# Reordering and padding the SBUF pools of a fused attention and two-MLP kernel so that the fp32r matmul operands lie at one address modulo 512 bytes

## The chip, the cores and the metric

The kernel runs on one NeuronCore of a Trainium2 chip. The metric is the device time of one execution in microseconds (us), from the chip's own clock; the median of several runs counts. TensorE is called PE, VectorE DVE, ScalarE ACT, GpSimd POOL, and SyncE SP.

## What is computed

The reference is causal attention with a sliding window and a few sink keys, followed by two MLPs without residuals. All inputs are float32.

```python
# q, k, v: (2, 8, 768, 64); n_sink 4, window 128
scores = q @ k.T / 8, kept where key < n_sink or 0 <= query - key < window, else -1e9
a = softmax(scores);  x = (a @ v) as (1536, 512)
h = x @ w_in                      # 512 -> 2048
x = (relu(h) ** 2) @ w_out        # 2048 -> 512
h = x @ w_in2
P = a0 + a1*h + a2*h**2 + a3*h**3
Q = 1 + |b0|*|h| + |b1|*h**2
out = (P / (Q + 1e-6)) @ w_out2
```

## The kernel before

**Precision.** Nearly every matrix product is made of three matmuls of type fp32r. Each operand is split into a high part (the value rounded to fp32r) and a low part (what is left of it), and the sum hi·hi + lo·hi + hi·lo is accumulated in PSUM. So a weight tile `w` becomes `whi` and `wlo`, the activations `x` become `xhi` and `xlo`, the hidden values `g` become `ghi` and `glo`, and the input `y` of the second MLP becomes `yhi` and `ylo`.

**Stages.** Tokens go through attention and the first MLP in four groups (`GROUPS`) of 512, 256, 256 and 512 tokens. While the MLP of one group runs on PE, the attention of the next group is woven into it (`slot`, `tick`). The last group has no attention beside it. Then the second MLP runs over three tiles of 512 tokens.

For each of the 16 blocks `f` of 128 hidden features, `gemm1_part` (L445 to L447) makes `h` with a 128x128 piece of the weights as the stationary operand, which PE loads before the matmul, and the activations as the moving operand, which streams through it: 12 matmuls of n columns, where n is the group's token number or 512. In the first MLP `gemm2a` (L468, L469, L472) follows, again with weights stationary and `ghi` or `glo` moving: 12 matmuls of n columns. In the second MLP `gemm2b` (L503 to L505) has it the other way round: pieces of `ghi` and `glo` are stationary, and the weights, 512 columns, are moving. Every one of these matmuls loads its stationary operand anew, and the load for a matmul is made while the matmul before it streams.

All in all there are 1,920 such matmuls of 512 columns and 768 of 256 columns. From the first matmul of the last token group to the end of the program PE has 1,548 matmuls, of which 1,536 have 512 columns and 12 have 256, left over from the third group.

**Order.** The order of the instructions on each engine is fixed when the program is built: by the scheduler, or, for PE in the two groups of 256 tokens, by the order of the code. In the part that runs here, this order is the same before and after the change on every engine, and so are the semaphores that each instruction waits for. (The two programs differ only in waits of the class `General`, a fallback for other inputs that does not run here.)

**Where tiles lie.** SBUF tiles come from pools, which are laid out one behind the other: `const` (masks, small constants) first, then `wp` (all 64 weight tiles of 2,048 bytes per partition), `stage` (raw weights from HBM, `st`; float32 weights, `wt`), `yp` (y, and early attention inputs), `xp` (`xhi`, `xlo`) and `gp` (`ghi`, `glo`) from the left, `att` (attention) and later `ysp` (`yhi`, `ylo` of the first and third tile; those of the second tile are in `xp`) from the right. A tile of `stage` with tag `st` is 4,104 bytes long, and three of them stand in a row, so what comes behind `stage` lies at another place modulo 512 than what comes before it. Slices of an operand step by 512 bytes (a piece of stationary operand), 1,024 or 2,048 bytes, so that each slice lies at its tile's address modulo 512.

Of the kernel before, what the change touches and what calls it, by code (L numbers as in the profile page):

```python
# [10 lines left out]
F32 = mybir.dt.float32  # L11
# [8 lines left out]
P = 128  # L20
# [27 lines left out]
TAIL = 3  # L48
HP = 60
NTOP = 1  # L50
IAD = 3
ST_T = 5
ST_PV = 2
# [18 lines left out]
def units():  # L72
    out = []
    for g, segs in enumerate(GROUPS):
        for h in range(H):
            xo = 0
            for seg in segs:
                out.append((g, h, seg, xo))
                xo += seg[2] * P
    return out  # L80
# [40 lines left out]
def to_f32(nc, st, t, top):  # L121

    mid = st.bitcast(I32)[:, 1 : 1 + 2 * WH].rearrange("p (n w) -> p n w", w=2)[:, :, 0]
    head = st.bitcast(BF16)[:, 4 : 4 + 4 * WH].rearrange("p (n w) -> p n w", w=4)[:, :, 0]
    nc.scalar.copy(top.bitcast(F16).rearrange("p (n w) -> p n w", w=2)[:, :, 1], head)  # L127
    nc.vector.scalar_tensor_tensor(t.bitcast(I32), in0=mid, scalar=13, in1=top,  # L128
                                   op0=ALU.logical_shift_right, op1=ALU.bitwise_or)
# [20 lines left out]
class Fast:  # L150
# [17 lines left out]
    def setup(self):  # L168
        nc, c = self.nc, self.const
        self.zero = c.tile([P, P], BF16, name="zero")  # L170
        nc.gpsimd.memset(self.zero, 0.0)
        self.tops = [c.tile([P, WH], I32, name=f"top{i}") for i in range(NTOP)]
        self.conv_i = 0
        for top in self.tops:
            nc.gpsimd.memset(top, 0)
        self.ident = c.tile([P, P], F32, name="ident")
        self.nsw = c.tile([P, 4], I32, name="nsw")
        self.nswf = c.tile([P, 4], F32, name="nswf")
        self.par = c.tile([P, 2], F32, name="par")
        ab = c.tile([P, 6], F32, name="ab")  # L180
        self.ab = ab
        io = self.io
        nc.scalar.dma_start(self.nsw, io["nsw"].bitcast(I32).partition_broadcast(P))
        nc.scalar.dma_start(ab[:, 0:4], io["a"].partition_broadcast(P))
        nc.scalar.dma_start(ab[:, 4:6], io["bb"].partition_broadcast(P))
        make_identity(nc, self.ident)
        rel = self.wp.tile([P, WH], F32, tag="whi4_0", name="rel")[:, :P]
        col = self.wp.tile([P, WH], F32, tag="wlo4_0", name="col")[:, :P]
        nc.gpsimd.iota(rel, pattern=[[-1, P]], base=0, channel_multiplier=1,
                       allow_small_or_imprecise_dtypes=True)  # L190
        nc.gpsimd.iota(col, pattern=[[1, P]], base=0, channel_multiplier=0,
                       allow_small_or_imprecise_dtypes=True)
        v = nc.vector
        f = self.nswf
        t = c.tile([P, 2], F32, name="neg")
        v.tensor_copy(f, self.nsw)
        lo = f.rearrange("p (s w) -> p s w", w=2)[:, :, 0:1]
        hi = f.rearrange("p (s w) -> p s w", w=2)[:, :, 1:2]
        t3 = t.rearrange("p (s w) -> p s w", w=1)
        p3 = self.par.rearrange("p (s w) -> p s w", w=1)  # L200
        v.tensor_scalar(t3, lo, 0.0, 4294967296.0, op0=ALU.is_lt, op1=ALU.mult)
        v.tensor_tensor(t3, t3, lo, op=ALU.add)
        v.scalar_tensor_tensor(p3, in0=hi, scalar=4294967296.0, in1=t3, op0=ALU.mult, op1=ALU.add)
        ns, win = self.par[:, 0:1], self.par[:, 1:2]
        self.m0 = c.tile([P, P], F32, name="m0")
        self.m1 = c.tile([P, 2 * P], F32, name="m1")
        self.m2 = c.tile([P, KB + P], F32, name="m2")
        self.nabs = c.tile([P, 2], F32, name="nabs")
        m0, m1, m2 = self.m0, self.m1, self.m2
        tmp = lambda tag: self.wp.tile([P, WH], F32, tag=tag, name="tmp")[:, :P]  # L210
        out, fut, rel1 = tmp("whi4_1"), tmp("wlo4_1"), tmp("whi5_0")
        v.tensor_scalar(fut, rel, 0.0, BIG, op0=ALU.is_lt, op1=ALU.mult)
        v.tensor_scalar_add(rel1, rel, 128.0)
        cur, prv = m2[:, KB : KB + P], m2[:, 0:P]
        v.tensor_scalar(cur, rel, win, BIG, op0=ALU.is_ge, op1=ALU.mult)
        v.tensor_tensor(cur, cur, fut, op=ALU.max)
        v.tensor_scalar(out, col, ns, BIG, op0=ALU.is_ge, op1=ALU.mult)
        v.tensor_tensor(m0, cur, out, op=ALU.min)
        v.tensor_scalar(prv, rel1, win, BIG, op0=ALU.is_ge, op1=ALU.mult)
        v.tensor_tensor(m1[:, 0:P], prv, out, op=ALU.min)  # L220
        v.tensor_copy(m1[:, P : 2 * P], cur)
        v.tensor_copy(m2[:, P:KB], out[:, :NSK])
        nu = sum(u[2][2] for u in units())
        self.mn = c.tile([P, nu], F32, name="mn")
        self.mn_i = 0


    def alt_tags(self, alt):
# [27 lines left out]
    def att_unit(self, u, raws, alt):  # L256
# [11 lines left out]
        at = self.att  # L268
# [19 lines left out]
            A.copy(vst[:, :, 0:D], vr3)  # L288
            G.tensor_tensor(vst[:, :, D : 2 * D], vr3, vst[:, :, 0:D].bitcast(F32), op=ALU.subtract)
        yield  # L290
        ps, sums = [], at.tile([P, 4], F32, tag="sums", name="sums", bufs=6)
        for i in range(nb):
            blk = blk0 + i
            if pv:
# [74 lines left out]
        c, half = h // 2, h % 2  # L369
# [43 lines left out]
    def w_split(self, which, f, half):  # L413
        with ExitStack() as c:
            if which == 0 and self.va_hist:
                for op in self.va_hist[-min(len(self.va_hist), 1 + IAD)]:
                    if op is not None:
# [3 lines left out]
    def w_split_(self, which, f, half):  # L421
        nc = self.nc
        st = self.wst.pop((which, f, half))
        t = self.stage.tile([P, WH], F32, tag="wt", name="wt", bufs=2)
        to_f32(nc, st, t, self.tops[self.conv_i % NTOP])
        self.conv_i += 1
# [81 lines left out]
    def run(self, ctx):  # L508
# [5 lines left out]
        mk = lambda c, name, bufs, side, **kw: c.enter_context(  # L514
            tc.tile_pool(name=name, bufs=bufs, side=side, reuse_waits="tile", **kw))
        root = ctx
        self.wp = mk(root, "wp", 1, "left")
        self.stage = mk(root, "stage", 1, "left")
        self.yp = mk(root, "yp", 1, "left")
        self.psum = mk(root, "psum", 1, None, space=bass.MemoryType.PSUM)  # L520
        self.att_banks, self.h_banks = [0, 1, 2, 3, 6, 7], [4, 5]
# [6 lines left out]
        sx = ExitStack()  # L528
        self.xp = mk(root, "xp", 1, "left")
        self.gp = mk(sx, "gp", 3, "left")  # L530
        sa = ExitStack()
        self.att = mk(sa, "att", 1, "right")

# [467 lines left out]
```

## Time and profile before

| | |
|---|---|
| median of 3 runs | 687.15 us (686.5 to 687.27) |
| the profiled execution's own time | 687.72 us |
| its span, first to last instruction | 685.8 us |
| PE busy | 661.7 us, 96% of the span |
| DVE / ACT / POOL busy | 509.8 / 475.6 / 164.0 us |
| granted PE clock, mean | 0.990 of full speed |

The span is what the trace covers; about 1.9 us of the execution lie around it. A row of the timeline is one instruction, or several of one line that follow each other, with its start and its duration. Matmuls overlap: the next one starts long before the one before it has ended, so what a matmul costs in a dense stretch is the distance from its start to the next start, not its duration. That distance is called its spacing here.

### The profile page before, as it was taken

The page shows a single profiled execution, that of the slowest core. Times are in us where ns is not written, and L with a number is a line of the kernel's source. Part 1 is how long each engine was busy: PE and PEld are TensorE (multiplying, and loading weights), DVE is VectorE, ACT ScalarE, POOL GpSimd, SP SyncE. Part 2 cuts the span into 40 slices and gives each one's busy share as a digit, 9 for nine tenths or more (in the row PEclk, how much of TensorE's full clock was granted, in tenths as well). Part 3 has the DMA queues.
Part 4 walks back from the last instruction along what each step waited for, and adds up shares of the span by engine and source line. Part 5 has one row for each costly group of instructions (what it writes and reads, how often), then busy time and mean ns, then how long its engine had stood idle before and what let it go on. Part 6 is the DMA issues. An engine that isn't in the chain of part 4 may idle for free.

```text
span 685.8 us, 10158 instructions
## 1 busy us (share of the span) xinstructions
PE 661.7 (96%) x3433; PEld 545.6 (80%) x3433; DVE 509.8 (74%) x1068; ACT 475.6 (69%) x1044; POOL 164.0 (24%) x174
## 2 busy tenths in 40 slices
PE   5999999999799999999999999999999999999995
PEld 3656787778699989999888888888888888888884
DVE  6886777778588887876566639998778778777772
ACT  4876977778677776766677758777666666666662
POOL 3553111111223232323000001353223332222221
PEclk9999999999799999999999999999999999999999
DMA  7761655445322222200456530000010000000001
GB/s 284 249 197 41 183 177 163 153 155 170 110 76 87 87 63 84 87 9 1 156 185 191 189 108 1 0 1 0 1 62 0 1 0 1 32 31 1 0 1 66
DMA packets 25403, 58.41 MB, mean 85 GB/s; under 512 B 3200, under 2 KB 9600, under 8 KB 25344
## 3 DMA queue, kind: packets, MB, share of 16 engines
q1 hardware_dynamic: 24768, 57.55, 26.4%
q8 instruction: 29, 0.48, 0.3%
q14 instruction: 30, 0.25, 0.1%
q10 hardware_dynamic: 576, 0.14, 0.1%
HBM read 54.53 MB, written 3.15 MB: 84 GB/s over the span
## 4 chain that ended last, share of the span: by engine, by line
PE 72%; DVE 0%; ACT 0%; issue 0%
PE b L445 11%; PE b L446 11%; PE b L447 11%; PE b L503 7%; PE b L505 7%; PE b L504 7%; PE b L468 4%; PE b L472 4%; PE b L469 4%; PE b L366 2%; PE b L303 2%; PE b L332 1%; PE b L357 1%; PE b L336 1%; PE b L656 0%
## 5 line engine op out<-in xcount | busy, mean ns | idle before, releaser
L445 PE MATMUL b<-xhi,whi 128*128 128x512 f32 (+1 forms) x320 | 112.5, 356 | 1.1 <-ACT xhi L374 0.8
L446 PE MATMUL b<-xlo,whi 128*128 128x512 f32 (+1 forms) x320 | 113.1, 354 | 0.0
L447 PE MATMUL b<-xhi,wlo 128*128 128x512 f32 (+1 forms) x320 | 112.5, 351 | 0.0
L494 POOL TENSOR_TENSOR glo<-t,ghi 128x512 fp32r<-128x512 f32 x34 | 45.0, 1323 | 220.4 <-ACT ghi L493 202.6
L468 PE MATMUL b<-ghi,whi 128*128 128x512 f32 (+1 forms) x256 | 77.8, 344 | 0.3 <-ACT b L456 0.3
L469 PE MATMUL b<-ghi,wlo 128*128 128x512 f32 (+1 forms) x256 | 76.8, 339 | 0.0
L504 PE MATMUL b<-wlo,ghi 128*128 128x512 f32 x192 | 76.0, 396 | 0.0
L503 PE MATMUL b<-whi,ghi 128*128 128x512 f32 x192 | 75.8, 396 | 0.0
L505 PE MATMUL b<-whi,glo 128*128 128x512 f32 x192 | 73.2, 396 | 0.0
L445 PEld LDWEIGHTS b<-xhi,whi 128*128 128x128 f32 x320 | 60.6, 190 | 9.8 <-ACT xhi L374 1.0
L447 PEld LDWEIGHTS b<-xhi,wlo 128*128 128x128 f32 x320 | 60.7, 190 | 9.0 <-DVE wlo L430 0.5
L446 PEld LDWEIGHTS b<-xlo,whi 128*128 128x128 f32 x320 | 60.9, 190 | 8.2
L282 POOL TENSOR_TENSOR klo<-raw,khi 128x448 fp32r<-128x448 f32 (+1 forms) x32 | 33.8, 1056 | 128.7 <-PE b L303 113.4
L430 DVE TENSOR_TENSOR wlo<-wt,whi 128x512 fp32r<-128x512 f32 x64 | 44.8, 700 | 24.7 <-ACT whi L429 24.3
L309 ACT ACTIVATE p<-p,mn 128x288 f32<-128x288 f32 (+2 forms) x96 | 48.3, 503 | 19.2 <-DVE mn L307 18.6
L429 ACT CAST whi<-wt 128x512 fp32r<-128x512 f32 x64 | 39.4, 616 | 29.0 <-PE b L446 23.2
L472 PE MATMUL b<-glo,whi 128*128 128x512 f32 (+1 forms) x256 | 57.0, 340 | 0.2 <-DVE glo L457 0.2
L307 DVE CUSTOM_DVE_ANT_0 p<-b,m 128x288 f32<-128x288 f32 (+2 forms) x96 | 39.6, 419 | 21.5 <-PE b L303 20.4
L128 DVE SCALAR_TENSOR_TENSOR wt<-st,top 128x512 int32<-128x512 int32 x64 | 48.1, 752 | 6.5 <-ACT top L127 4.7
L469 PEld LDWEIGHTS b<-ghi,wlo 128*128 128x128 f32 x256 | 47.8, 188 | 5.7 <-DVE wlo L430 0.5
L468 PEld LDWEIGHTS b<-ghi,whi 128*128 128x128 f32 x256 | 47.5, 188 | 5.8 <-ACT b L456 0.6
L445 PE MATMUL b<-yhi,whi 128*128 128x512 f32 x128 | 50.7, 396 | 0.0
(151 smaller groups left out, 1554.3 us busy)
## 6 DMA issues: line engine op xcount, KB each, us to landing
st<-w SPq DMA_DIRECT2D x64, 512.0 KB, 3.8
raw<-att SPq DMA_DIRECT2D x24, 352.0 KB, 2.9
rawv<-att SPq DMA_DIRECT2D x32, 128.0 KB, 2.4
raw<-att SPq DMA_DIRECT2D x12, 256.0 KB, 3.6
raw_e<-att SPq DMA_DIRECT2D x8, 352.0 KB, 4.6
out<-o SPq DMA_DIRECT2D x8, 256.0 KB, 2.3
rawv<-att SPq DMA_DIRECT2D x16, 64.0 KB, 2.7
raw_e<-att SPq DMA_DIRECT2D x4, 256.0 KB, 5.0
```

The source lines that it names most:

```text
L128: nc.vector.scalar_tensor_tensor(t.bitcast(I32), in0=mid, scalar=13, in1=top, op0=ALU.logical_shift_right, op1=ALU.bitwise_or)
L309: self.lastA = A.activation(pt[:, :w], pt[:, :w], AF.Exp, scale=-1.0, bias=mn, accum_out=sums[:, i : i + 1])
L445: nc.tensor.matmul(h[:, :n], whi[:, cs], xhi[:, c, :n], start=(c == 0), stop=False)
L446: nc.tensor.matmul(h[:, :n], whi[:, cs], xlo[:, c, :n], start=False, stop=False)
L447: nc.tensor.matmul(h[:, :n], wlo[:, cs], xhi[:, c, :n], start=False, stop=(c == NC - 1))
L468: nc.tensor.matmul(acc[m], whi[:, ms], ghi, start=(f == 0 and not pk), stop=pk, **kw)
L469: nc.tensor.matmul(acc[m], wlo[:, ms], ghi, start=False, stop=pk, **kw)
L472: nc.tensor.matmul(acc[m], whi[:, ms], glo, start=False, stop=pk or f == NF - 1, **kw)
L494: self.lastL = nc.gpsimd.tensor_tensor(glo, t3, ghi.bitcast(F32), op=ALU.subtract)
L503: nc.tensor.matmul(acc[t], ghi[:, ts_], whi, start=(f == 0), stop=False)
L504: nc.tensor.matmul(acc[t], ghi[:, ts_], wlo, start=False, stop=False)
L505: nc.tensor.matmul(acc[t], glo[:, ts_], whi, start=False, stop=(f == NF - 1))
```

## The change

```diff
+PAD = 128
 ...
 # Fast.setup
         self.mn = c.tile([P, nu], F32, name="mn")
         self.mn_i = 0
+        c.tile([P, PAD // 4], F32, name="pad")
 ...
 # Fast.att_unit
-        ps, sums = [], at.tile([P, 4], F32, tag="sums", name="sums", bufs=6)
+        ps, sums = [], self.const.tile([P, 4], F32, tag="sums", name="sums", bufs=6)
 ...
 # Fast.run
         self.wp = mk(root, "wp", 1, "left")
-        self.stage = mk(root, "stage", 1, "left")
         self.yp = mk(root, "yp", 1, "left")
 ...
         self.xp = mk(root, "xp", 1, "left")
         self.gp = mk(sx, "gp", 3, "left")
+        self.stage = mk(sx, "stage", 1, "left")
```

A tile of 128 bytes that nothing uses is put behind the constants, the six small `sums` tiles (32 bytes apart) move from `att` to `const`, and the pool `stage` moves behind `gp`. No instruction is added, removed or moved. What changes is where tiles lie. From the allocation of the two built programs, addresses in a partition modulo 512:

| operand | before | after |
|---|---|---|
| `whi`, `wlo` (all weight tiles) | 160 | 480 |
| `xhi`, `xlo`; `yhi`, `ylo` of the second tile | 256 | 480 |
| `ghi`, `glo` | 256 | 480 |
| `yhi`, `ylo` of the first and third tile | 480 | 480 |
| attention `khi`, `vst`, `pst`, `pthi`, `ptlo` | 480 | 480 |
| attention `klo` | 224 | 224 |
| attention `qst` | 288 | 480 |
| attention `raw` (two buffers) | 288, 32 | 480, 224 |
| attention `p` (four buffers) | 480, 96, 224, 352 | the same |
| `st` (three buffers) | 160, 192, 224 | 480, 0, 32 |
| `wt` | 256 | 64 |

## Rows read from the trace of the kernel before

**Rows 1.** The page: PE's busy time, and the span in 40 slices.

```profile
PE 661.7 (96%) x3433; PEld 545.6 (80%) x3433; DVE 509.8 (74%) x1068; ACT 475.6 (69%) x1044; POOL 164.0 (24%) x174
...
PE   5999999999799999999999999999999999999995
...
PEclk9999999999799999999999999999999999999999
```

**Rows 2.** Busy time of each engine by stretch (us); instructions in brackets; PE clock.

```profile
core 0: us, PE busy (x) PEld busy (x) DVE busy (x) ACT busy (x) POOL busy (x), PEclk, DMA share, GB/s
...
70.00:171.70 101.70, 100.80 (x483) 80.30 (x482) 78.70 (x168) 80.21 (x174) 13.84 (x14) 1.00 0.54 166
171.70:184.30 12.60, 8.16 (x34) 6.97 (x34) 6.28 (x24) 7.36 (x21) 2.44 (x4) 0.59 0.39 119
184.30:318.50 134.20, 133.05 (x1077) 127.79 (x1076) 103.09 (x304) 93.97 (x285) 36.29 (x41) 1.00 0.22 66
318.50:409.60 91.10, 91.10 (x398) 73.61 (x397) 55.46 (x82) 62.32 (x111) 5.73 (x4) 1.00 0.49 156
409.60:678.10 268.50, 268.50 (x1153) 216.60 (x1151) 213.89 (x301) 182.11 (x314) 75.96 (x60) 1.00 0.02 9
...
440.00:480.00 40.00, 40.00 (x173) 32.27 (x172) 37.32 (x51) 30.95 (x56) 17.85 (x15) 1.00 0.00 1
```

**Rows 3.** The timeline of PE: first matmul of the last token group, last of all.

```profile
318.46 0.48 PE L445 MATMUL b<-xhi,whi 128*128 128x512 f32 x1
...
678.09 0.40 PE L505 MATMUL b<-whi,glo 128*128 128x512 f32 x1
```

**Rows 4.** Timeline, moving operand at 256, weights at 160: first and last of 43 starts.

```profile
330.06 0.39 PE L447 MATMUL b<-xhi,wlo 128*128 128x512 f32 x1
...
339.86 0.39 PE L445 MATMUL b<-xhi,whi 128*128 128x512 f32 x1
```

**Rows 5.** Timeline, weights moving at 160, hidden values stationary at 256: eight starts.

```profile
455.18 0.39 PE L504 MATMUL b<-wlo,ghi 128*128 128x512 f32 x1
...
456.34 0.40 PE L503 MATMUL b<-whi,ghi 128*128 128x512 f32 x1
456.58 0.40 PE L504 MATMUL b<-wlo,ghi 128*128 128x512 f32 x1
456.82 0.39 PE L505 MATMUL b<-whi,glo 128*128 128x512 f32 x1
```

**Rows 6.** Timeline, y moving at 480, weights at 160: one slow and one fast stretch.

```profile
457.05 0.40 PE L445 MATMUL b<-yhi,whi 128*128 128x512 f32 x1
...
459.85 0.39 PE L503 MATMUL b<-whi,ghi 128*128 128x512 f32 x1
...
426.02 0.39 PE L447 MATMUL b<-yhi,wlo 128*128 128x512 f32 x1
...
428.08 0.40 PE L447 MATMUL b<-yhi,wlo 128*128 128x512 f32 x1
```

**Rows 7.** Timeline, L505 followed by L445 (160 and 160): first and last pair of 40.

```profile
430.89 0.39 PE L505 MATMUL b<-whi,glo 128*128 128x512 f32 x1
431.12 0.40 PE L445 MATMUL b<-yhi,whi 128*128 128x512 f32 x1
...
664.06 0.39 PE L505 MATMUL b<-whi,glo 128*128 128x512 f32 x1
664.29 0.40 PE L445 MATMUL b<-yhi,whi 128*128 128x512 f32 x1
```

**Rows 8.** Timeline, L447 followed by L503, second tile (256 and 256): first and last pair of 15.

```profile
493.25 0.39 PE L447 MATMUL b<-xhi,wlo 128*128 128x512 f32 x1
493.49 0.39 PE L503 MATMUL b<-whi,ghi 128*128 128x512 f32 x1
...
577.36 0.39 PE L447 MATMUL b<-xhi,wlo 128*128 128x512 f32 x1
577.59 0.39 PE L503 MATMUL b<-whi,ghi 128*128 128x512 f32 x1
```

**Rows 9.** Timeline, L447 followed by L503, other tiles (480 and 256): last pair of 26.

```profile
666.85 0.40 PE L447 MATMUL b<-yhi,wlo 128*128 128x512 f32 x1
667.09 0.39 PE L503 MATMUL b<-whi,ghi 128*128 128x512 f32 x1
```

**Rows 10.** Timeline, 256 columns, moving at 256, weights at 160; then attention at 480 and 480.

```profile
221.06 0.28 PE L445 MATMUL b<-xhi,whi 128*128 128x256 f32 x1
...
223.33 0.28 PE L469 MATMUL b<-ghi,wlo 128*128 128x256 f32 x1
...
224.73 0.50 PE L366 MATMUL b<-ptlo,vst 128*128 128x128 f32 x3
225.07 0.62 PE L332 MATMUL b<-ident,p 128*128 128x128 f32 x4
```

**Rows 11.** Who PE waited for: all of 184.30 to 318.50 us, then timeline at 172 us.

```profile
PE b L357 <- DVE pst L347: 1.0, 1, 1.0
...
171.64 0.34 PE L366 MATMUL b<-ptlo,vst 128*128 128x256 f32 x2
174.53 0.58 PE L303 MATMUL b<-khi,qst 128*128 128x256 f32 x1 [2.55 <-DVE qst L283]
```

## The prediction

> **What bounds the kernel now.** I read the page first. PE is busy for 96% of the span, at tenths of 9 in nearly every slice, and at full clock but for one slice in the first third and the last one [rows 1]. By stretches, PE has no idle time to speak of from 70 us to 171.7 us, waits for 1.0 us in all between 184.3 us and 318.5 us, and not at all from there to 678.1 us; the other engines are at 80% or less over each of these stretches [rows 2, 11]. So the kernel is a queue of matmuls, and its time is their number times their spacing. A change that moves no instruction can then do one thing that counts: alter the spacing. What other engines do faster or slower is hidden under PE as long as they keep up.
>
> So I looked at the spacing itself. From the first matmul of the last group, at 318.46 us, to the last matmul of all, at 678.09 us, there are 1,547 spacings in 359.63 us [rows 3]. Twelve of them belong to matmuls of 256 columns, at some 119.5 ns; the other 1,535 take (359.63 - 1.43) us / 1,535 = 233.35 ns each. That is a mean over very regular patterns. The starts in the trace are in whole nanoseconds though the timeline prints hundredths of a us, and I worked out each spacing from them, together with the places of the two operands that PE reads at the time: the moving operand of the matmul that streams, and the stationary operand of the next one, which is being loaded meanwhile.
> - Moving at 256, loaded at 160: 42 spacings in 9.80 us, 233.3 ns [rows 4]. In nanoseconds they repeat 231, 232, 237.
> - Moving at 160, loaded at 256 (second MLP, `gemm2b`): seven spacings in 1.64 us, 234.3 ns, from 231 up to 238 [rows 5].
> - Moving at 480, loaded at 160 (second MLP, `gemm1`): mostly 233.3 ns (twelve in 2.80 us), but in one stretch nine in 2.06 us, 228.9 ns [rows 6].
>
> What speaks for the change is in the places where both operands happen to have one address modulo 512 already. Where the last L505 of a block is followed by L445, weights stream from 160 while weights at 160 are loaded: 40 such pairs, mean 230.9 ns, none under 230 or over 233 [rows 7]. Where L447 is followed by L503 in the second tile, it is 256 and 256: 15 pairs, mean 230.1, from 229 to 231 [rows 8]. The same two lines in the other two tiles, with `y` at 480 against 256, take 233.1 ns as a mean of 26 pairs, which spread from 229 to 235 [rows 9]. Same lines, same shapes, same neighbours; only the place of `y` differs. So the spacing does depend on the two places, and equal ones sit at the low end of what unequal ones show.
>
> The Trainium skill speaks against this (SBUF — State Buffer, "Who interferes with whom"): it gives PE two read ports, one for the moving operand and one for the weight load, calls them independent, and says that PE never waits on anyone. By that rule the place of an operand could not matter and the change would be worth nothing; the pairs just shown, 230.1 against 233.1 ns, do not agree with it.
>
> **The change part by part.** After it every pair in the MLPs is an equal one, 480 and 480.
>
> *Matmuls of 512 columns after 318.46 us.* I take 230.5 ns, between the two kinds of equal pair (230.9 and 230.1). 1,535 x (233.35 - 230.5) = 4.4 us. The best bound is the fast stretch, 228.9 ns: 6.8 us. The other bound is a loss, below.
>
> *The other 384 of 512 columns*, in the first group, stand among attention matmuls, in a stretch where PE is as dense [rows 2]. With the spacing of rows 4 they would give 384 x 2.8 = 1.1 us; I count 0.8, because some stand next to matmuls of the attention, whose operands are not all moved to 480. What PE saves there does pass on: after 171.7 us PE waits for DVE's `qst` [rows 11], which is made when PE has let go of the buffers of the unit before.
>
> *Matmuls of 256 columns.* Nineteen spacings in 2.27 us, 119.5 ns [rows 10], with 256 and 160. No pair of this shape has equal places. The nearest row has: three attention matmuls of 128, 256 and 128 columns, all operands at 480, in 0.34 us, 113 ns each [rows 10]. I take 116, between the two, since these are shorter on average. Of 768 such matmuls some 700 are followed by another of the kind: 700 x 3.5 = 2.4 us. Bounds: 113 ns gives 4.6 us, 119.5 ns nothing. PE is the bound here too: one wait of 1.0 us in 134.2 us [rows 2, 11].
>
> *Attention.* `qst` goes from 288 to 480 and `raw` from 288 and 32 to 480 and 224; the large operands were at 480 before. I count nothing: these matmuls are short, and many stand in the first 70 us, where PE is not the bound.
>
> *Everything else.* `sums`, the padding and the moved `stage` add no instruction and no wait. DVE, ACT, POOL and the DMAs get other addresses; no row tells what that does to them, but PE covers it. The tightest cover is between 440 and 480 us, where DVE is busy for 37.32 of 40 us [rows 2]. With PE 1.2% faster that becomes 37.3 of 39.5, still under PE. Were DVE late there, what is lost is what PE gains in these 40 us, 0.5 us.
>
> Sum: 4.4 + 0.8 + 2.4 = 7.6 us. Against the profiled execution, 687.72 us, that is 680.1; the median of the runs is 0.6 us lower, so the forecast for the median is 687.15 - 7.6 = 679.6 us. With the good bounds everywhere, 6.8 + 4.6 + 1.7 (384 x 4.45), it is 13.1 us, and 674.0.
>
> **The rivals.** *Nothing changes.* The equal pairs are single ones, each with an unequal pair before and behind it. The spacings come in patterns that repeat over several matmuls (231, 232, 237), so a single one of 231 proves little about a steady run: the 237 may come anyway, as it does after two of 231 with unequal places. Then the mean stays near 233.3 and the time at 687.15 us. For it: the pattern of rows 4. Against it: 55 equal pairs without one spacing over 233, where a third of 237s would have shown some 18. It would be the outcome, too, if only the distance of successive operands mattered and not the pair.
>
> *Slower: equal places are the worst ones.* If both reads begin in the same place at the same time, in every matmul, one may hold up the other every time. The single equal pairs come out of a run of unequal ones, so their reads may be out of step; in a steady run they would fall into step and stay there. The price is the longest spacing that is common now, 238 ns (0.24 us in rows 5): 1,535 x 4.65 = 7.1 us, 384 x 4.65 = 1.8 us, and 2% of 119.5 ns on 700 others, 1.7 us: 10.6 us, and 697.8 us. It decides from the point where the steady spacing is over 233.35 ns. For it speaks that attention, at 480 and 480, is not strikingly quick; against it, again, that no equal pair is over 233 ns.
>
> *Faster than forecast.* The fast stretch of rows 6 shows that 228.9 ns can be held for nine matmuls. If equal places hold it for good, it is the 674.0 us above.
>
> *The clock.* After PE's idle time at 172 us [rows 11] it runs for some 10 us at the lower of its two levels: the mean is 0.59 of 2.4 GHz in the 12.6 us to 184.3 us [rows 2]. If the idle time falls otherwise, this stretch could be shorter or longer. At full clock the 12.6 us, of which PE is busy for 8.16, would be some 2.5 us shorter. That belongs to the range of each case and to none alone.
>
> **How the numbers follow.** The forecast, a gain of 4.5 to 12 us, gets 0.66: the pairs are many and sharp, but single. Nothing, or a gain of under 4.5 us, gets 0.16; slower 0.11; faster than by 12 us, with the best spacing or the clock, 0.07. The range goes from 674.0, the good bounds, to 687.0, just under no change: it leaves out the slower case, most of the case of no change at all, and a little at the lower end, together under 2 in 10. A measurement of this kernel tells some 0.2%, 1.4 us, from no change. Faster by more than that takes in the forecast, the greater gain and a part of the small gains: 0.79. The same: 0.10. Slower: 0.11.
>
> **What would show it.** The two matmuls that enclose the last 1,548 should lie 355 us apart instead of 359.6, and the spacings in the second MLP should be an even 229 to 231 ns, without the 237s. The stretch with the 256-column matmuls, 134.2 us now, should be 2 to 3 us shorter, with PE still waiting for 1 to 2 us there. If the spacing of the 512-column matmuls stays at 233, the forecast is wrong at its root; if it is over 234, equal places are bad. If the spacing falls and the time does not, the gain has gone into waits of PE, first in 184.3 to 318.5 us (for `pst` and `pthi`), then for `glo` in 440 to 480 us.

## The result

The changed kernel takes 676.2 us (median of 4 runs, 675.0 to 676.5) against 687.0 us (4 runs, 686.5 to 687.3): a ratio of 0.984, 95% interval 0.982 to 0.986. That is a gain of 10.8 us. Timed once more, beside the experiments, it was 675.9 against 687.4 us, ratio 0.983 (0.981 to 0.985).

The page after, the lines that answer to [rows 1], and with them the costliest matmul of the second MLP and a DVE group that reads and writes moved tiles, which has the same 44.8 us and 700 ns on the page of before (columns: busy us, mean ns of one, idle before):

```profile
PE 648.8 (96%) x3433; PEld 543.9 (81%) x3433; DVE 509.0 (76%) x1068; ACT 475.3 (71%) x1044; POOL 163.5 (24%) x174
...
PE   5999999999799999999999999999999999999995
...
PEclk9999999999799999999999999999999999999998
...
L505 PE MATMUL b<-whi,ghi 128*128 128x512 f32 x192 | 74.4, 389 | 0.0
...
L432 DVE TENSOR_TENSOR wlo<-wt,whi 128x512 fp32r<-128x512 f32 x64 | 44.8, 700 | 22.3 <-ACT whi L431 21.9
```

PE is the only engine whose busy time has changed by more than 2 us: 648.8 us after 661.7, with the same 3,433 instructions in the trace. Its weight loads (PEld) take 1.7 us less in all; DVE, ACT and POOL are within 1 us of before, although most of their tiles lie elsewhere now. (Lines of `kernel.py` are one or two higher after the change: L447 to L449 are the L445 to L447 of before, L505 to L507 the L503 to L505.)

Busy time by stretch after (PE, PEld, DVE, ACT, POOL, granted clock, DMA). The cuts follow those of [rows 2], to within a few instructions; the second one lies where the clock has risen again, and that comes earlier after the change:

```profile
70.00:169.80 99.80, 98.77 (x480) 80.07 (x479) 78.25 (x168) 79.73 (x173) 13.62 (x14) 1.00 0.55 168
169.80:180.80 11.00, 6.36 (x28) 5.09 (x27) 5.93 (x22) 6.04 (x18) 2.41 (x4) 0.69 0.43 141
180.80:315.70 134.90, 133.76 (x1083) 128.60 (x1082) 103.13 (x306) 95.03 (x289) 35.97 (x41) 1.00 0.22 65
315.70:403.50 87.80, 87.80 (x395) 72.90 (x393) 55.49 (x82) 62.41 (x111) 5.73 (x4) 1.00 0.52 162
403.50:665.40 261.90, 261.90 (x1157) 216.80 (x1156) 213.74 (x301) 182.29 (x314) 76.03 (x60) 1.00 0.02 9
```

PE still has no idle time in the last two rows, and in the third of them the waits view knows the one wait of [rows 11]:

```profile
PE b L359 <- DVE pst L349: 1.0, 1, 1.0
```

The timeline of PE after shows where the time went: the start of the last attention matmul before PE's idle time, the first matmul after the low clock, the first and the last of the last 1,548 matmuls, and a stretch of the second MLP:

```profile
169.82 0.34 PE L368 MATMUL b<-ptlo,vst 128*128 128x256 f32 x2
...
181.54 0.28 PE L447 MATMUL b<-xhi,whi 128*128 128x256 f32 x1
...
315.73 0.48 PE L447 MATMUL b<-xhi,whi 128*128 128x512 f32 x1
...
665.35 0.39 PE L507 MATMUL b<-whi,glo 128*128 128x512 f32 x1
...
447.98 0.39 PE L505 MATMUL b<-whi,ghi 128*128 128x512 f32 x1
...
450.70 0.39 PE L447 MATMUL b<-yhi,whi 128*128 128x512 f32 x1
...
453.42 0.39 PE L505 MATMUL b<-whi,ghi 128*128 128x512 f32 x1
```

The last stretch takes 665.35 - 315.73 = 349.62 us, where [rows 3] had 359.63: 10.0 of the 12.6 us by which the span shrank. From 447.98 to 453.42 there are 24 spacings in 5.44 us, 226.7 ns each, through `gemm2b` and `gemm1` alike; in nanoseconds they are 226 or 227, and the 231, 232, 237 of [rows 4] is gone. The other 2.6 us: 1.8 before the idle time (its last matmul starts at 169.82, after 171.64 in [rows 11]), 0.7 in the idle and low-clock stretch up to the same matmul (181.54 - 169.82 = 11.72 us; before, the matmul at 184.09 us, 12.45 us), 0.2 from there to the last group; and 0.1 is lost at the end. The mean clock in that stretch is 0.69 after 0.59, which comes to some 6.8 us at the lower of the two levels (1.2 GHz) after and 10.3 us before. That this is the change's doing is not shown: a kernel of the last experiment, traced twice, has a mean clock of 0.90 and of 0.85 from 165 to 200 us, the same two values as the kernels after and before. So the 0.7 us can come and go from run to run.

### The profile page after: what moved, and what is told of

Its sections match the earlier page's. It is cut to its first block, busy times and chain, and to the rows that moved or that the text cites. A ratio compares the mean times of both kernels' runs of the same rounds, so it can differ in the third digit from the quotient of the medians.

```text
span 673.2 us, 10158 instructions
## 1 busy us (share of the span) xinstructions
PE 648.8 (96%) x3433; PEld 543.9 (81%) x3433; DVE 509.0 (76%) x1068; ACT 475.3 (71%) x1044; POOL 163.5 (24%) x174
## 4 chain that ended last, share of the span: by engine, by line
PE 72%; DVE 0%; ACT 0%; issue 0%
PE b L447 11%; PE b L449 11%; PE b L448 11%; PE b L505 6%; PE b L507 6%; PE b L506 6%; PE b L470 4%; PE b L474 4%; PE b L471 4%; PE b L368 3%; PE b L305 2%; PE b L334 1%; PE b L359 1%; PE b L338 1%; PE b L658 0%
## 5 line engine op out<-in xcount | busy, mean ns | idle before, releaser
L447 PE MATMUL b<-xhi,whi 128*128 128x512 f32 (+1 forms) x320 | 111.5, 353 | 1.1 <-ACT xhi L376 0.8
L448 PE MATMUL b<-xlo,whi 128*128 128x512 f32 (+1 forms) x320 | 111.9, 350 | 0.0
L449 PE MATMUL b<-xhi,wlo 128*128 128x512 f32 (+1 forms) x320 | 111.6, 349 | 0.1
L505 PE MATMUL b<-whi,ghi 128*128 128x512 f32 x192 | 74.4, 389 | 0.0
L507 PE MATMUL b<-whi,glo 128*128 128x512 f32 x192 | 71.9, 389 | 0.0
L447 PEld LDWEIGHTS b<-xhi,whi 128*128 128x128 f32 x320 | 60.7, 191 | 8.5 <-ACT xhi L376 1.0
L449 PEld LDWEIGHTS b<-xhi,wlo 128*128 128x128 f32 x320 | 61.0, 191 | 8.0 <-DVE wlo L432 0.5
L448 PEld LDWEIGHTS b<-xlo,whi 128*128 128x128 f32 x320 | 61.0, 191 | 7.3
L432 DVE TENSOR_TENSOR wlo<-wt,whi 128x512 fp32r<-128x512 f32 x64 | 44.8, 700 | 22.3 <-ACT whi L431 21.9
L474 PE MATMUL b<-glo,whi 128*128 128x512 f32 (+1 forms) x256 | 56.2, 337 | 0.2 <-DVE glo L459 0.2
L128 ACT CAST top<-st 128x512 f16<-128x512 bf16 x64 | 49.6, 775 | 1.2 <-DVE wt L129 1.1
```

The source lines that it names most:

```text
L447: nc.tensor.matmul(h[:, :n], whi[:, cs], xhi[:, c, :n], start=(c == 0), stop=False)
L448: nc.tensor.matmul(h[:, :n], whi[:, cs], xlo[:, c, :n], start=False, stop=False)
L449: nc.tensor.matmul(h[:, :n], wlo[:, cs], xhi[:, c, :n], start=False, stop=(c == NC - 1))
L474: nc.tensor.matmul(acc[m], whi[:, ms], glo, start=False, stop=pk or f == NF - 1, **kw)
L505: nc.tensor.matmul(acc[t], ghi[:, ts_], whi, start=(f == 0), stop=False)
L507: nc.tensor.matmul(acc[t], glo[:, ts_], whi, start=False, stop=(f == NF - 1))
```

## The experiments

All start from the changed kernel. The spacings below are means over all pairs of neighbouring matmuls in the trace of which both are of the lines and the size named, from their starts in nanoseconds; the few over 260 ns (512 columns) or 160 ns (256), at a wait or a change of stage, are left out.

### How near must the addresses be, and modulo what?

A pad between the weight pool and the pools of `x` and `g`, of 256, 128, 64 and 32 bytes:

```diff
+        gap = mk(root, "gap", 1, "left")
+        gap.tile([P, 256 // 4], F32, name="gap")
         self.yp = mk(root, "yp", 1, "left")
```

> After the change, with a pad of 256 bytes put between the weight pool and the pools of x and g, so that x and g (and y of the second tile) lie at 224 modulo 512, weights and y of the other tiles at 480. Theory A (only equality modulo 512 counts): the spacing of the 512-column matmuls of the last token group and of the second tile goes from 226.7 ns to 233 to 234, in L505 to L507 too; L447 to L449 in the first and third tile keep 226.7; time about 685 us. Theory B (the period is 256 bytes or a divisor of it): every spacing stays 226.7 and the time stays 675 to 676.5 us.

> The same with a pad of 128 bytes: x and g at 96, weights at 480. Theory A: 233 to 234 ns for the moved pairs, about 685 us. Theory B with a period of 128 bytes or less: 226.7 ns everywhere, 675 to 676.5 us. If 256 bytes leave 226.7 and 128 bytes do not, the period is 256.

> The same with a pad of 64 bytes: x and g at 32, weights at 480. Theory A: 233 to 234 ns for the moved pairs, about 685 us. Theory B with a period of 64 bytes: 226.7 ns, 675 to 676.5 us. Theory C (a small distance is as good as none, as it is the meeting of the two reads in time that counts): between 226.7 and 233 ns, nearer the first than with 128 bytes.

> The same with a pad of 32 bytes, the smallest: x and g at 0, weights at 480. Theory A: 233 to 234 ns for the moved pairs, about 685 us. Theory C: still close to 226.7 ns, and the time under 680 us. The two directions are told apart by the stage: moving operand 32 bytes ahead of the loaded one in the last token group, 32 bytes behind it in L505 to L507.

| pad | L447 to L474, last group and second tile (x, g moving) | L505 to L507 (weights moving) | L447 to L449, first and third tile (equal) | 256 columns | one run, us |
|---|---|---|---|---|---|
| 0 (the change) | 226.8 | 226.6 | 226.6 | 119.4 | 675.0 |
| 256 | 226.8 | 226.6 | 226.7 | 119.4 | 675.9 |
| 128 | 232.6 | 233.0 | 229.3 | 118.8 | 685.0 |
| 64 | 229.5 | 233.4 | 229.2 | 117.4 | 682.6 |
| 32 | 233.3 | 233.1 | 227.3 | 117.0 | 682.8 |
| before: 96, and other y | 233.5 | 234.1 | 232.0 | 119.7 | 687.7 |

The first and last matmul of the last stretch with 256 bytes:

```profile
316.31 0.49 PE L447 MATMUL b<-xhi,whi 128*128 128x512 f32 x1
...
665.96 0.39 PE L507 MATMUL b<-whi,glo 128*128 128x512 f32 x1
```

and with 128 bytes:

```profile
317.98 0.48 PE L447 MATMUL b<-xhi,whi 128*128 128x512 f32 x1
...
675.59 0.40 PE L507 MATMUL b<-whi,glo 128*128 128x512 f32 x1
```

That is 349.65 and 357.61 us. With 256 bytes between the operands nothing of the 10.0 us is lost, with 128 bytes four fifths of it. So what counts is equality modulo 256 bytes, not 512: theory B with that period, and theory A in all but its modulus. Theory C is out: 32 bytes already cost some 6.5 ns. Only the moving operand 64 bytes ahead is cheaper, 229.5 ns. The 685 us of theory A came with 128 bytes alone; 64 and 32 bytes ended at 682.6 and 682.8, as some of their columns in the table are shorter.

The fourth column is the answer to a question that the forecast got wrong. In the first and third tile L447 to L449 have equal places in all these kernels except the one before, and take 226.7 ns only where `gemm2b`, with which they alternate every 12 matmuls, is equal too. Beside unequal neighbours the same equal pairs take 227.3 to 229.3 ns. One such run of twelve with 128 bytes, its first, eighth and twelfth start:

```profile
478.16 0.40 PE L447 MATMUL b<-yhi,whi 128*128 128x512 f32 x1
...
479.78 0.39 PE L448 MATMUL b<-ylo,whi 128*128 128x512 f32 x1
...
480.69 0.40 PE L449 MATMUL b<-yhi,wlo 128*128 128x512 f32 x1
```

The first seven spacings take 1.62 us, 231 ns each, the last four 0.91 us, 227 ns each. So it goes in all such runs of these traces: with 128 bytes the means by place in the run lie between 225.9 and 235.3 ns for the first seven spacings and between 226.7 and 227.4 from the eighth on; with 64 bytes the first six are uneven; with 32 bytes only the first is long, 230.9 ns, and the others are 227.3 or less. So an unequal pair costs something in the matmuls behind it as well, in up to seven of them here, and a run of equal pairs settles at 226.7.

### One part of the change alone

`stage` behind `g`, but no pad, and `sums` in `att` as before. Everything of the MLPs then lies at 160, except for `y` of the first and third tile, at 480:

```diff
-        c.tile([P, PAD // 4], F32, name="pad")
 ...
-        ps, sums = [], self.const.tile([P, 4], F32, tag="sums", name="sums", bufs=6)
+        ps, sums = [], at.tile([P, 4], F32, tag="sums", name="sums", bufs=6)
```

> One part of the change alone: the stage pool moves behind g, without the pad and with sums where they were. Weights, x and g then all lie at 160, y of the first and third tile at 480 as before, which is 64 bytes off modulo 256. If equality counts and not the address itself: 226.7 ns in the last token group and in the second tile; in the first and third tile 229 to 234 ns; time 678 to 681 us. If 480 itself counts: above 230 ns everywhere and about 685 us.

It took 678.8 us beside 687.5, as expected. The first and last matmul of the last stretch:

```profile
316.84 0.48 PE L446 MATMUL b<-xhi,whi 128*128 128x512 f32 x1
...
669.25 0.39 PE L506 MATMUL b<-whi,glo 128*128 128x512 f32 x1
```

That is 352.41 us, 7.2 of the 10.0 us of the whole change. The last group and the second tile have 227.1 and 226.7 ns in L446 to L448, at 160: it is not the address 480 that counts. The first and third tile have 230.4 ns there. `gemm2b`, which is unequal in none of its pairs, takes 226.7 ns in the second tile, among equal neighbours, and 230.2 in the other two. Within one program the same lines thus differ only where `y` lies elsewhere, which leaves little room for another cause, such as the other engines' new addresses. So the moved pool alone brings some 8.7 us in this run, and the pad and `sums`, which only bring `y` into line, the last 2 to 3 us.

### Which two operands?

All low parts 96 bytes behind the high parts, with pools of their own, so that the low part of the moving operand streams while the low part of the weights is loaded:

```diff
-PAD = 128
+PAD = 32
+GAP = 96
 ...
+        mk(sx, "gap", 1, "left").tile([P, GAP // 4], F32, name="gap")
+        self.wpl = mk(sx, "wpl", 1, "left")
+        self.xpl = mk(sx, "xpl", 1, "left")
+        self.gpl = mk(sx, "gpl", 3, "left")
         self.stage = mk(sx, "stage", 1, "left")
 ...
```

(The lines left out put `wlo`, `xlo`, `glo` and `ylo` into these places.)

> After the change, with every low part 96 bytes behind its high part modulo 512: whi, xhi, ghi, yhi at 384, wlo, xlo, glo, ylo at 480. This tells apart which two operands have to be equal. Theory P (the moving operand of the matmul that streams, and the stationary operand of the next one, loaded meanwhile): in the order hi-hi, lo-hi, hi-lo of L445 to L447 and of L503 to L505 these two are always equal, so the spacing in the second MLP stays 226.7 ns; in the first MLP L468 (ghi moving, wlo loaded) and L472 (glo moving, whi loaded) are unequal, so some 230 to 233 ns in those; time 676 to 678 us. Theory O (the two operands of one matmul): two of three matmuls of each triple are unequal, so 231 to 234 ns everywhere, and 682 to 686 us.

680.9 us: between the two theories. The timeline of the second MLP, seven starts, and the first and last matmul of the last stretch:

```profile
455.14 0.39 PE L451 MATMUL b<-yhi,whi 128*128 128x512 f32 x1
455.37 0.39 PE L452 MATMUL b<-ylo,whi 128*128 128x512 f32 x1
455.60 0.39 PE L453 MATMUL b<-yhi,wlo 128*128 128x512 f32 x1
455.82 0.39 PE L451 MATMUL b<-yhi,whi 128*128 128x512 f32 x1
456.06 0.39 PE L452 MATMUL b<-ylo,whi 128*128 128x512 f32 x1
456.29 0.39 PE L453 MATMUL b<-yhi,wlo 128*128 128x512 f32 x1
456.51 0.39 PE L451 MATMUL b<-yhi,whi 128*128 128x512 f32 x1
...
317.12 0.48 PE L451 MATMUL b<-xhi,whi 128*128 128x512 f32 x1
...
671.30 0.39 PE L511 MATMUL b<-whi,glo 128*128 128x512 f32 x1
```

Two triples in 1.37 us are 228 ns a matmul. The triple of `gemm1` is 230.9, 232.0 and 224.4 ns in the first and third tile, 229.1 on average, and that of `gemm2b` 231.0, 231.4 and 224.6. The last stretch takes 671.30 - 317.12 = 354.18 us. Then the low parts of the weights alone, 96 bytes off:

```diff
+GAP = 96
 ...
+        mk(sx, "gap", 1, "left").tile([P, GAP // 4], F32, name="gap")
+        self.wpl = mk(sx, "wpl", 1, "left")
         self.stage = mk(sx, "stage", 1, "left")
 ...
```

> After the change, with the low parts of the weights alone moved by 96 bytes (576 modulo 512, that is 64), all else at 480. In L445 to L447 of the MLPs the moving operand stays at 480 throughout; only the stationary one of L447 is elsewhere. Theory P (moving operand of one matmul against the loaded one of the next): the long spacing is the one from L446 to L447, in which wlo is loaded, and L468 to L469; the others of the triple stay at 226 to 227 ns, the mean is about 229 ns. Theory O (the two operands of one matmul): the long one is from L447 to L445, in which wlo is in use, and L469 to L468. Theory S (a chain of starts, in which each change of place of a stream shifts the next start): both neighbours change, one longer and one shorter. Time about 679 to 682 us in each.

This took 685.3 us, more than any theory had said. First and last matmul of the last stretch:

```profile
318.25 0.48 PE L451 MATMUL b<-xhi,whi 128*128 128x512 f32 x1
...
675.81 0.39 PE L511 MATMUL b<-whi,glo 128*128 128x512 f32 x1
```

357.56 us: one weight operand of three in another place loses eight tenths of what the change had brought there. The three spacings of the triple are 233.1, 232.1 and 232.6 ns in the first and third tile; none of them stands out and none is shorter than in the changed kernel, so none of the three theories finds its mark. By the count of unequal pairs within one matmul (theory O), the first kernel has two of three and the second one of three, and the first should be the slower; it is the faster by 3.4 us in the last stretch. By the count of a streaming operand against the one being loaded (theory P), it is none against one of three, and the order is right. But P alone gives 226.7 for the first, and it has 229.1. Nor does P show within the first kernel: in its last token group `gemm2a`, unequal by P in eight spacings of twelve, has 230.6 ns, and `gemm1`, unequal in none, 231.6, though its neighbours may have a part in that. So which two operands have to be equal stays open, and so does what a change of place from one matmul to the next costs. In the second kernel every third pair is unequal, and a run would not have the seven matmuls in which it could settle; that fits its loss, but was not tested. A rule that gives all these numbers was not found.

### Are 256 columns different?

The table shows that matmuls of 256 columns are shortest where those of 512 are not: 117.0 ns with 32 bytes, 119.4 with none. Their tiles are half empty, so `x` and `g` of the two groups of 256 tokens can be shifted inside them without any other tile moving:

```diff
+XOFF = 32 // 4
+GOFF = 32 // 4
 ...
 # Fast.new_x
+        o = XOFF if GN[g] <= 256 else 0
 ...
-            self.xp.tile([P, w], F32R, tag=k, name=k)[:, : NC * GN[g]] ...
+            self.xp.tile([P, w], F32R, tag=k, name=k)[:, o : o + NC * GN[g]] ...
 ...
 # act1
-        ghi = self.gp.tile([P, n], F32R, tag="ghi", name="ghi")
 ...
+        o = GOFF if n <= 256 else 0
+        ghi = self.gp.tile([P, n + o], F32R, tag="ghi", name="ghi")[:, o:]
```

(`glo` likewise; the ends of the two `xp` lines are left out.)

> After the change, with x and g of the two groups of 256 tokens moved 32 bytes inside their tiles, so that only the matmuls of 256 columns have their moving operand 32 bytes ahead of the loaded one. With 32 bytes for all they had 117.0 ns as against 119.4 with equal places, while those of 512 columns lost. If the two sizes are independent: 117 ns for 256 columns, 226.7 for 512, some 1.6 us less than the changed kernel: 673.5 to 674.9 us. If 117 came from the neighbours or from another operand: 119.4 and about 676 us.

> The same with x of the two groups of 256 tokens moved by 16 bytes and g by 48, to see how fine the places count. If places count in steps of 32 bytes or more: L445 to L447 at 119.4 ns as with 0, L468 to L472 near 117 as with 32 and 64. If finer: other values, between 113 and 120 ns. Time 673 to 676 us.

With 32 bytes one block of the timeline, first and last of 20 starts:

```profile
218.10 0.28 PE L450 MATMUL b<-xhi,whi 128*128 128x256 f32 x1
...
220.32 0.28 PE L475 MATMUL b<-ghi,wlo 128*128 128x256 f32 x1
```

and the same block of the changed kernel:

```profile
218.51 0.28 PE L447 MATMUL b<-xhi,whi 128*128 128x256 f32 x1
...
220.78 0.28 PE L471 MATMUL b<-ghi,wlo 128*128 128x256 f32 x1
```

2.22 against 2.27 us, 116.8 against 119.5 ns; the 512-column matmuls keep their 226.7 ns. The run took 673.7 us, and the forecast of two independent sizes came true. With 16 bytes for `x` the matmuls of `gemm1` take 117.6 ns on average, and with 48 bytes for `g` those of `gemm2a` 118.3, at 674.95 us: places count in steps finer than 32 bytes, and 32 is the best of those tried. Timed:

> The changed kernel again, beside the kernel before and the next one on one chip: 676.2 us, ratio 0.984; spacing of 512 columns after the attention 226.7 ns.

> The kernel with x and g of the two groups of 256 tokens at 32 bytes from the weights, timed: if the gain of the one look is real, 1.3 to 2 us under the changed kernel beside it, ratio to before 0.981 to 0.982. If the look had caught only a shorter stretch at low clock: no difference to the changed kernel over 0.5 us.

On one chip, with the same runs of the kernel before (687.4 us): the changed kernel 675.9 us, ratio 0.983 (0.981 to 0.985); with the shift 674.3 us, ratio 0.980 (0.979 to 0.982). The 1.6 us between them are near the 1.7 us that 700 x 2.4 ns come to, and it is the best version here; but the two intervals overlap a little, so the difference between the two rests on the spacings more than on the times.

## Why the prediction was right, and where its terms were off

- **The bound** was read rightly. PE was a gapless queue, the busy time of DVE, ACT and POOL stayed within 1 us, and a shorter spacing came out in the time without a new wait: PE's waits between 180.8 and 315.7 us are the same 1.0 us for `pst`, and none follow.
- **That equal places are short** was read rightly from a few dozen pairs in the trace of before. The rule of the Trainium skill (SBUF — State Buffer, "Who interferes with whom"), that PE's two read ports are independent and PE waits for nobody, would leave no room for this. These matmuls do not bear it out: the same instructions take 226.7 or 233 ns by the place of their operands alone. What happens inside PE or its memory stays open.
- **The term of the 512 columns was mis-sized.** Predicted 230.5 ns and 4.4 us; measured (349.62 - 1.43) / 1,535 = 226.8 ns and 10.0 us, with the last stretch at 349.62 us where 355 were forecast. Even the bound that was called the best, 228.9, was passed. The step that failed is taking single equal pairs for a steady run of them. The rival "nothing changes" rightly said that the pattern spans several matmuls, but the pattern worked the other way: the single pairs of [rows 7, 8] were too long because of their unequal neighbours. The table's fourth column and the runs that settle show the same: with 128 and 32 bytes the first equal pair behind unequal ones takes 235.3 and 230.9 ns, and a run that has settled 226.7.
- **The first group's 384** were put at 0.8 us. Their own spacing fell from 233.6 to 228.6 ns over 321 pairs, 1.6 us, for the same reason; in all, 1.8 us were gained by the last matmul before PE's idle time.
- **Attention** was put at nothing, and at most some 0.2 us of these 1.8 is left for it. The table of addresses leaves out that the first attention units keep a part of `khi`, `klo`, `qst`, `pst` and `pthi` in weight tiles, which went from 160 to 480 with the weights. That PE is not the bound in the first 70 us was read too coarsely, too: from 17 to 70 us it is busy for 50.1 of 53.0 us. Little hung on either.
- **The term of the 256 columns was wrong.** Predicted 116 ns and 2.4 us; measured 119.4 to 119.5 ns and 0.2 us. The step that failed is taking the three attention matmuls of 113 ns, of 128, 256 and 128 columns, for a near row, and carrying the finding at 512 columns over to 256. At 256 columns equal places are no better than those of before; 32 bytes off are.
- **The sum** of 7.6 us came out as 10.8, and 679.6 us as 676.2, still in the range because the good bounds were in it. The terms of 512 columns were too small by 5.6 and about 1 us, that of 256 columns too large by 2.2: that the sum came this near is in part luck. In the two profiled executions, 687.72 and 675.02 us, the terms add up to 12.0 of 12.7 us, and most of the rest is the stretch of low clock.
- **The rival of slower** fell: no steady run of equal places showed a spacing near 238 ns.

## What to carry to other kernels

Where PE runs without gaps, look at the distance from start to start of its matmuls in nanoseconds: a pattern that repeats over a few matmuls is a loss that can depend on where operands lie. For fp32r matmuls of 512 columns that load new weights each time, put all moving and stationary operands at one address modulo 256 bytes; all of them, since one weight operand in three elsewhere gave most of the gain back, and an unequal pair lengthens equal ones behind it. Don't carry the finding to another size without measuring: 256 columns wanted 32 bytes of distance.

## What was not expected of the hardware

- The period is 256 bytes: 226.8 ns with 256 bytes of distance, 232.6 with 128.
- After unequal pairs a run of equal ones takes up to seven matmuls to settle at 226.7 ns (128 bytes), or one (32 bytes).
- At 512 columns unequal places cost up to some 7.5 ns a matmul on average (234.1 against 226.6). At 256 columns, equal places hold the spacing mostly on 120 ns, and places 32 bytes apart, at a mixture of 113 to 120, bring the mean to 117.
- The Trainium skill (TensorE: Matmul & The Clock Gate, "Back-to-back issue gap") gives N / 2.4 + 2.5 ns for an isolated matmul of N columns at full clock, by which 512 columns would take an estimated 215.8 ns; what it gives for a stream of them is lower still. No kind of pair in any run here has a mean under 224 ns. What keeps even equal places 11 ns above that estimate stays open.
